# Retention attention feeding a Swish feed-forward block: regrouping a chunk's products and writing two heads into the halves of one bank

## The chip, the cores and the metric

The kernel runs on one core of a Trainium2 chip. The metric is device time in microseconds (us). The profiler records one execution; its instructions are named by engine: PE (TensorE, matrix products), PEld (its weight loads), DVE (VectorE), ACT (ScalarE), POOL (GpSimd) and SP (the queue that issues most DMAs).

## The reference

```python
# q, k, v: [8 batches, 8 heads, 576 positions, 64]
scale = 1.0 / np.sqrt(D_)
scores = scale * np.matmul(q, k.transpose(0, 1, 3, 2))
gamma = 1.0 - 2.0 ** (-5.0 - np.arange(H, dtype=np.float32))
rel = pos[:, None] - pos[None, :]
Dmat = np.where(rel >= 0, gamma[:, None, None] ** rel[None, :, :], 0.0)
attn = np.matmul(scores * Dmat, v)
x = attn.transpose(0, 2, 1, 3).reshape(B * S, H * D)   # [4608, 512]
h = x @ w_in                                           # [4608, 2048]
out = (h * (1.0 / (1.0 + np.exp(-beta * h)))) @ w_out  # [4608, 512]
```

There is no softmax: the decay splits into a factor of the query's position and one of the key's, so a running state per head carries all earlier positions.

## The kernel before

**The two halves.** The feed-forward half works on 9 blocks of 512 tokens. `up` (L277) multiplies one 128-wide slice of the hidden layer: four products of 512 columns into a bank of tag `mm` (three banks), then a Silu on ACT. `down` (L290) adds four of the 16 products of one 128-token output tile in a bank of the same tag; after the last, DVE copies it out (L302) and SP stores it. A block is 16 steps of `up` and 16 of `down`, each of four products. The attention half works on 40 chunks (8 batches of four chunks of 128 positions and one of 64); all 8 heads of a chunk are done together, in four pairs of 64+64 rows.

**A chunk's steps.** `pre` (L169) scales q and v by the decay and casts k to bf16, on POOL from chunk 4 on (L182, L186, L187). v goes into one of three padded tiles `vpads`: each head has 128 columns there, its 64 own ones at the side that belongs to it in the pair and zeros at the other. `load_next` (L191) asks SP for the three loads of the chunk seven further on. q and k are then transposed, up to chunk 13 by `a_T` (L205: eight PE transposes and an ACT copy, L216), from chunk 14 on by `a_X` (L195), a DMA transpose issued from ACT's queue that goes through the crossbar. `a_sc` (L219) makes the scores: eight products of 64 rows, the two heads of a pair in the upper and the lower half of the PE array (L228); DVE masks them into `R` (L232). `a_st` (L256) adds four products to the state (L266), which ACT copies to `sbd`, two heads on a block diagonal (L272). `a_O` (L235) makes the output in one bank: four products of the state before with q (L244), then eight of `vpads` with `R`, each 128 wide with one half zeros (L249); DVE copies the sum to `xT` (L253), which `up` reads.

**The order.** It is written by hand. [...] A list `fill` of `up` and `down` steps is merged with timed steps of the chunks: `merged` (L307) puts a step with time t ahead of fill step number t, rounded up. `attn_steps` (L320) gives the times of a chunk whose time is `at`, with `gap` = 2:

```python
if i < XB:      # XB = 14
    return [(at - 4, F(pre, i)), (at - 3.9, F(load_next, i)), (at, F(a_T, i)), (at + gap, F(a_sc, i)),
            (at + 2 * gap, F(a_st, i)), (at + 2 * gap, F(a_O, i))]
return [(at - 10, F(pre, i)), (at - 9.9, F(load_next, i)), (at - 5, F(a_X, i)), (at + gap, F(a_sc, i)),
        (at + 2 * gap, F(a_st, i)), (at + 2 * gap, F(a_O, i))]
```

So scores come two steps after `at`, state and output two steps after the scores. Chunks 0 to 6 have places written out one by one (L328 to L368), 7 and 8 stand at 23 and 27 of the second list. From chunk 9 on the chunks that block m+1 needs are spread over the 32 steps of block m, four or five to a block; the first such stretch begins at `n1`, where the second part of block 1's `up` begins, with products of 320 columns.

Buffers: `qk` and `qkT` rotate over four, `R` and `sbd` over two, `vpads` over three, the loaded tiles over seven; scores have two banks, output, state and PE transposes one each.

Of the kernel before, what the change touches and what calls it, by code (L numbers as in the profile page):

```python
# [12 lines left out]
BF16 = mybir.dt.bfloat16  # L13
ACT = mybir.ActivationFunctionType
ALU = mybir.AluOpType
# [4 lines left out]
def kernel(  # L20
# [10 lines left out]
    nc = tc.nc  # L31
    B, H, S, D = q.shape
# [3 lines left out]
    P = 128  # L36
    HP = H // 2
    KO = d_model // P
    FO = d_ff // P
    MB = 512  # L40
    NMB = N // MB
# [4 lines left out]
    consts = ctx.enter_context(tc.tile_pool(name="consts", bufs=1))  # L46
# [3 lines left out]
    sb = ctx.enter_context(tc.tile_pool(name="sb", bufs=2))  # L50
# [13 lines left out]
        qkv_tiles[(b, c)] = t  # L64

    NQ = 7
    XB = 14
    order = [(b, c) for b in range(B) for c in range(NC)]
    for b, c in order[:4]:
        load_chunk(b, c)  # L70
# [13 lines left out]
    for h in range(H):  # L84
# [11 lines left out]
    nc.gpsimd.affine_select(out=causal[:], in_=causal[:], pattern=[[1, P]], compare_op=ALU.is_ge,  # L96
                            fill=0.0, base=0, channel_multiplier=-1)

    NV = 3
    vpads = [consts.tile([P, H, P], BF16, name=f"vpad{i}") for i in range(NV)]  # L100

    NS = 2
    sbds = [consts.tile([P, HP, P], BF16, name=f"sbd{i}") for i in range(NS)]
    nc.gpsimd.memset(vpads[0][:], 0.0)
    nc.vector.memset(sbds[0][:], 0.0)
    nc.gpsimd.memset(vpads[1][:], 0.0)
    nc.vector.memset(sbds[1][:], 0.0)


# [57 lines left out]
    live = {}  # L167

    def pre(i):  # L169

        b, c = order[i]
        c0, cL = chunks[c]
        t = qkv_tiles.pop((b, c))
        first = i < 4
        qk = sb.tile([P, 2, H, D], BF16, name="qk", tag="qk", bufs=4)
        qn, kn = qk[:, 0], qk[:, 1]
        vp = vpads[i % NV]

        vp4 = vp.rearrange("p (pr two) (x d) -> p pr (two x) d", two=2, x=2)[:, :, 0::3, :]
        gq_b = gq[:cL, c, :].unsqueeze(2).to_broadcast([cL, H, D])  # L180
        gv_b = gv[:cL, c, :].unsqueeze(2).to_broadcast([cL, H, D])
        (nc.vector if first else nc.gpsimd).tensor_tensor(qn[:cL], t[:cL, 0], gq_b, ALU.mult)  # L182
        if first:
            nc.scalar.copy(kn[:cL], t[:cL, 1])
        else:
            nc.gpsimd.tensor_copy(kn[:cL], t[:cL, 1])  # L186
        nc.gpsimd.tensor_tensor(vp4[:cL], t[:cL, 2].rearrange("p (pr two) d -> p pr two d", two=2),  # L187
                                gv_b.rearrange("p (pr two) d -> p pr two d", two=2), ALU.mult)
        live[i] = dict(qk=qk, qn=qn, kn=kn, vp=vp, vp4=vp4)

    def load_next(i):  # L191
        if i + NQ < len(order):
# [12 lines left out]
    def a_T(i):  # L205
        b, c = order[i]
        c0, cL = chunks[c]
        L = live[i]
        T = psum.tile([P, 2, HP, P], BF16, name="T", tag="T", bufs=1)
        for j, src in enumerate((L["qn"], L["kn"])):  # L210
            for p in range(HP):
                nc.tensor.transpose(T[:, j, p, :cL],  # L212
                                    src[:cL, 2 * p:2 * p + 2, :].rearrange("p h d -> p (h d)"),
                                    ident[:cL, :cL])
        qkT = sb.tile([P, 2, HP, P], BF16, name="qkT", tag="qkT", bufs=4)
        nc.scalar.copy(qkT[:, :, :, :cL], T[:, :, :, :cL])  # L216
        L["qT"], L["kT"] = qkT[:, 0], qkT[:, 1]
# [17 lines left out]
    def a_O(i):  # L235
        b, c = order[i]
        c0, cL = chunks[c]
        L = live[i]
        R, vp = L["R"], L["vp"]
        O = psum.tile([P, HP, P], F32, name="O", tag="O", bufs=1)  # L240
        n = 0
        if c > 0:
            for p in range(HP):
                nc.tensor.matmul(O[:, p, :cL], sbds[(i - 1) % NS][:, p, :], L["qT"][:, p, :cL],  # L244
                                 start=(n == 0), stop=False, skip_group_check=True)
                n += 1
        for j in range(2):
            for p in range(HP):
                nc.tensor.matmul(O[:, p, :cL], vp[:cL, 2 * p + j, :], R[:cL, j, p, :cL],  # L249
                                 start=(n == 0), stop=(j == 1), skip_group_check=True)  # L250
                n += 1
        n0 = b * S + c0
        nc.vector.tensor_copy(xT[:, :, n0:n0 + cL], O[:, :, :cL])  # L253
        del live[i]

    def a_st(i):  # L256
        b, c = order[i]
        c0, cL = chunks[c]
        L = live[i]
        if c == NC - 1:  # L260
            return
        if c == 0:
            state_ps[b] = psum.tile([P, HP, P], F32, name="st", tag="st", bufs=1)
        st = state_ps[b]
        for p in range(HP):
            nc.tensor.matmul(st[:, p, :], L["kn"][:cL, 2 * p:2 * p + 2, :].rearrange("p h d -> p (h d)"),  # L266
                             L["vp4"][:cL, p], start=(c == 0 and p == 0), stop=True,
                             skip_group_check=True)
        sbd = sbds[i % NS]
        for j in range(2):  # L270
            r = slice(j * D, (j + 1) * D)
            nc.scalar.copy(sbd[r, :, j * D:(j + 1) * D], st[r, :, j * D:(j + 1) * D])  # L272
# [34 lines left out]
    def merged(fill, *streams):  # L307

        todo = sorted((x for st in streams for x in st), key=lambda x: x[0])
        for n, f in enumerate(fill):  # L310
            while todo and todo[0][0] <= n:
                todo.pop(0)[1]()
            f()
        for _, step in todo:
            step()

    def F(f, *a):
        return lambda: f(*a)

    def attn_steps(i, at, gap=2.0):  # L320

        if i < XB:
            return [(at - 4, F(pre, i)), (at - 3.9, F(load_next, i)), (at, F(a_T, i)), (at + gap, F(a_sc, i)),
                    (at + 2 * gap, F(a_st, i)), (at + 2 * gap, F(a_O, i))]
        return [(at - 10, F(pre, i)), (at - 9.9, F(load_next, i)), (at - 5, F(a_X, i)), (at + gap, F(a_sc, i)),
                (at + 2 * gap, F(a_st, i)), (at + 2 * gap, F(a_O, i))]

    warm_up(12)  # L328
    betas()
    pre(0)  # L330
    a_T(0)
    nc.gpsimd.memset(vpads[2][:], 0.0)
    pre(1)
    for i in range(4):
        warm_up(2)
        a_sc(i)
        a_st(i)
        if i < 3:
            a_T(i + 1)
            if i < 2:  # L340
                pre(i + 2)
        else:
            cast_w_in(0)
            warm_up(2)
        a_O(i)

    fill = [F(up, 0, fo) for fo in range(FO)]
# [5 lines left out]
    for i in range(5):  # L353
# [7 lines left out]
    fill = [F(up, 1, fo, 0, q1) for fo in range(FO)]  # L361
    fill += [F(down, 0, ms, f0) for f0 in range(0, FO, 4) for ms in range(3)]
    fill += [F(down, 0, 3, f0) for f0 in range(0, FO, 4)]
    n1 = len(fill)
    fill += [F(up, 1, fo, q1, MB - q1) for fo in range(FO)]
    fill += [F(down, 1, ms, f0) for ms in range(MB // P) for f0 in range(0, FO, 4)]
    streams = [[(4, F(cast_w_out, 0)), (10, F(cast_w_out, 1)), (18, F(cast_w_out, 2)), (21, F(cast_w_out, 3))],
               [(0, F(a_T, 6)), (4, F(a_sc, 6)), (8, F(a_st, 6)), (8, F(a_O, 6))],  # L368
               attn_steps(7, 23), attn_steps(8, 27)]
    done = 9  # L370
    need = lambda m: min(len(order), next((i + 1 for i, (b, c) in enumerate(order)
                                          if b * S + chunks[c][0] + chunks[c][1] >= (m + 1) * MB), len(order)))
    todo = list(range(done, need(2)))
    streams += [attn_steps(i, n1 + n * 30 / len(todo)) for n, i in enumerate(todo)]
    done = need(2)
    for m in range(2, NMB):
        base = len(fill)
        fill += [F(up, m, fo) for fo in range(FO)]
        fill += [F(down, m, ms, f0) for ms in range(MB // P) for f0 in range(0, FO, 4)]
        if m + 1 < NMB:  # L380
            todo = list(range(done, need(m + 1)))
            streams += [attn_steps(i, base + n * 31 / len(todo)) for n, i in enumerate(todo)]
            done = need(m + 1)
    merged(fill, *streams)


# [28 lines left out]
```

## Time and profile before

| What | us |
|---|---|
| median of the runs (3 runs: 326.5 to 329.17) | 327.55 |
| the profiled execution, its own time | 327.24 |
| its span, first to last instruction | 325.5 |
| PE busy | 311.7 (96%) |
| ACT busy | 141.6 (44%) |
| DVE busy | 114.4 (35%) |
| POOL busy | 113.3 (35%) |

A line of a timeline has the start, the time from first start to last end, engine, line, operation and count; consecutive equal instructions are merged. Products on PE are pipelined, so the end of a group overlaps the start of the next: what a group costs is the distance from its start to the next group's start. "PEld" rows are the weight loads. "ACTq" and "SPq" rows are DMA issues, and "to landing" is the time from such an issue until the data are there.

### The profile page before, as it was taken

What the parts mean: (1) busy time and instruction counts of PE and PEld (TensorE: products, weight loads), DVE (VectorE), ACT (ScalarE), POOL (GpSimd) and SP (SyncE); (2) the same over time, 40 slices, a digit from 0 to 9 for tenths busy, and PEclk for the clock granted to TensorE, in tenths of its full rate; (3) what the DMA queues carried; (4) which work ended last, traced back from release to release, by engine and by line L of the source; (5) the groups of instructions that cost most, each with busy time, mean ns of one, the idle gap of its engine ahead of it and who ended that gap; (6) DMA issues with size and microseconds to landing.
All of it is one profiled execution on the core that took longest, in us unless ns stands there. A gap on an engine that the chain in (4) does not pass through costs nothing.

```text
span 325.5 us, 5518 instructions
## 1 busy us (share of the span) xinstructions
PE 311.7 (96%) x2208; PEld 163.8 (50%) x2247; DVE 114.4 (35%) x202; ACT 141.6 (44%) x246; POOL 113.3 (35%) x132
## 2 busy tenths in 40 slices
PE   6779999999999999999999999999999999999995
PEld 2544584566555555544555555544545555544442
DVE  3685273634423244214423343224324432330011
ACT  2567881276237610760076106710662057305700
POOL 5323847974333354333333353333333430000000
PEclk9799999999999999999999999999999999999998
DMA  9999999999974999999999869656315121110011
GB/s 171 218 378 244 256 373 220 206 213 213 266 127 126 166 216 220 163 225 184 254 194 191 174 152 226 117 129 156 89 34 113 67 64 34 49 65 34 0 64 64
DMA packets 146362, 52.54 MB, mean 161 GB/s; under 512 B 137616, under 2 KB 137632, under 8 KB 146336
## 3 DMA queue, kind: packets, MB, share of 16 engines
q1 hardware_dynamic: 121920, 46.15, 63.8%
q10 hardware_dynamic: 24416, 6.04, 11.3%
q8 instruction: 17, 0.28, 0.4%
q14 instruction: 9, 0.07, 0.1%
HBM read 36.71 MB, written 9.44 MB: 142 GB/s over the span
## 4 chain that ended last, share of the span: by engine, by line
PE 91%; DVE 3%; DMA 2%; ACT 1%; issue 1%; ACTq 0%
PE po L296 38%; PE ph L284 37%; PE O L249 5%; PE sc L228 4%; PE st L266 2%; DMA qkT<-qk 2%; PE ph L152 2%; PE O L244 2%; PE T L212 2%; DVE R L232 1%; ACT qkT L216 1%; ACT sbd L272 0%; DVE xT L253 0%; DVE w_in_sb L130 0%; DVE tiny L160 0%
## 5 line engine op out<-in xcount | busy, mean ns | idle before, releaser
L284 PE MATMUL ph<-xT,w_in_sb 128*128 128x512 bf16 (+2 forms) x623 | 131.4, 357 | 2.5 <-DVE xT L253 1.6
L296 PE MATMUL po<-w_out_sb,gT 128*128 128x512 bf16 x556 | 130.2, 379 | 1.1 <-issue 0.2
L286 ACT ACTIVATE gT<-ph,beta_sb 128x512 bf16<-128x512 f32 (+2 forms) x160 | 101.9, 645 | 64.6 <-PE ph L284 48.2
L187 POOL TENSOR_TENSOR vpad<-qkvn,gv 128x512 bf16<-128x512 f32 (+1 forms) x40 | 42.0, 1051 | 135.9 <-issue 93.2
L284 PEld LDWEIGHTS <-w_in_sb 128*128 128x128 bf16 x640 | 59.1, 98 | 58.5 <-issue 1.6
L296 PEld LDWEIGHTS <-gT 128*128 128x128 bf16 x576 | 54.0, 98 | 60.6
L232 DVE TENSOR_TENSOR R<-sc,causal 128x512 bf16<-128x512 f32 (+1 forms) x80 | 47.2, 631 | 92.4 <-PE sc L228 92.2
L272 ACT CAST sbd<-st 64x256 bf16<-64x256 f32 x64 | 23.3, 364 | 77.2 <-PE st L266 76.4
L302 DVE COPY ot<-po 128x512 f32<-128x512 f32 x36 | 24.8, 691 | 66.1 <-PE po L296 63.9
L253 DVE CAST xT<-O 128x512 bf16<-128x512 f32 (+1 forms) x40 | 25.5, 637 | 38.2 <-PE O L249 38.2
L182 POOL TENSOR_TENSOR qk<-qkvn,gq 128x512 bf16<-128x512 f32 (+1 forms) x36 | 37.8, 1051 | 2.1 <-DMA qkvn<-in_q_dram 1.6
L249 PE MATMUL O<-R,vpad 128*128 128x128 bf16 (+1 forms) x320 | 23.5, 213 | 1.2 <-DVE R L232 1.2
L216 ACT COPY qkT<-T 128x1024 bf16<-128x1024 bf16 (+1 forms) x14 | 13.3, 950 | 21.8 <-PE T L212 21.7
L186 POOL CAST qk<-qkvn 128x512 bf16<-128x512 f32 (+1 forms) x36 | 21.9, 608 | 1.1 <-DMA qkvn<-in_k_dram 1.1
L249 PEld LDWEIGHTS <-vpad 128*128 128x128 bf16 (+1 forms) x320 | 18.2, 97 | 2.3 <-issue 1.8
L228 PEld LDWEIGHTS <-qkT 64*128 64x128 bf16 (+1 forms) x320 | 8.9, 98 | 17.7 <-issue 11.4
L228 PE MATMUL sc<-qkT 64*128 64x128 bf16 (+1 forms) x320 | 15.4, 217 | 0.9 <-ACT qkT L216 0.4
L266 PEld LDWEIGHTS <-qk 128*128 128x128 bf16 x128 | 9.5, 99 | 6.6 <-issue 0.2
L266 PE MATMUL st<-vpad,qk 128*128 128x128 bf16 x128 | 12.6, 222 | 0.1
L212 PE MATMUL T<-ident,qk 128*128 128x128 bf16 (+1 forms) x112 | 8.7, 224 | 3.1 <-DVE qk L182 3.0
L244 PE MATMUL O<-qkT,sbd 128*128 128x128 bf16 (+1 forms) x128 | 11.5, 212 | 0.0
L212 PEld LDWEIGHTS <-qk 128*128 128x128 bf16 (+1 forms) x112 | 7.2, 103 | 5.1 <-DVE qk L182 3.1
(38 smaller groups left out, 59.1 us busy)
## 6 DMA issues: line engine op xcount, KB each, us to landing
out_dram<-ot SPq DMA_DIRECT2D x36, 256.0 KB, 2.4
qkvn<-in_q_dram SPq DMA_DIRECT2D x32, 256.0 KB, 4.7
qkvn<-in_k_dram SPq DMA_DIRECT2D x32, 256.0 KB, 5.0
qkvn<-in_v_dram SPq DMA_DIRECT2D x32, 256.0 KB, 5.3
wt<-in_moe_w_in_dram SPq DMA_DIRECT2D x4, 1024.0 KB, 10.4
wt<-in_moe_w_out_dram SPq DMA_DIRECT2D x4, 1024.0 KB, 10.6
qkvn<-in_q_dram SPq DMA_DIRECT2D x8, 128.0 KB, 4.7
qkvn<-in_k_dram SPq DMA_DIRECT2D x8, 128.0 KB, 4.3
```

The lines of the kernel that those rows point to most:

```text
L182: (nc.vector if first else nc.gpsimd).tensor_tensor(qn[:cL], t[:cL, 0], gq_b, ALU.mult)
L187: nc.gpsimd.tensor_tensor(vp4[:cL], t[:cL, 2].rearrange("p (pr two) d -> p pr two d", two=2), gv_b.rearrange("p (pr two) d -> p pr two d", ...
L228: nc.tensor.matmul(sc[j][:cL, p, :cL], L["kT"][r, p, :cL], L["qT"][r, p, :cL], start=True, stop=True, skip_group_check=True)
L232: nc.vector.tensor_tensor(R[:cL, j, :, :cL], sc[j][:cL, :, :cL], m_b, ALU.mult)
L249: nc.tensor.matmul(O[:, p, :cL], vp[:cL, 2 * p + j, :], R[:cL, j, p, :cL], start=(n == 0), stop=(j == 1), skip_group_check=True)
L253: nc.vector.tensor_copy(xT[:, :, n0:n0 + cL], O[:, :, :cL])
L266: nc.tensor.matmul(st[:, p, :], L["kn"][:cL, 2 * p:2 * p + 2, :].rearrange("p h d -> p (h d)"), L["vp4"][:cL, p], start=(c == 0 and p == 0 ...
L272: nc.scalar.copy(sbd[r, :, j * D:(j + 1) * D], st[r, :, j * D:(j + 1) * D])
L284: nc.tensor.matmul(ph[:, :tn], w_in_sb[:, ko, fo * P:(fo + 1) * P], xT[:, ko, x0:x0 + tn], start=(ko == 0), stop=(ko == KO - 1))
L286: nc.scalar.activation(gT[:, fo, t0:t0 + tn], ph[:, :tn], ACT.Silu, scale=beta_sb[:, fo:fo + 1])
L296: nc.tensor.matmul(po[:], gT[:, fo, ms * P:(ms + 1) * P], w_out_sb[:, fo, :], start=(fo == 0), stop=(fo == FO - 1))
L302: nc.vector.tensor_copy(ot, po[:])
```

## The change

1. **Padded v is gone.** `vpads`, its three memsets and the strided write are removed. `pre` writes v into `vn`, [128, 8 heads, 64], from a pool of four. `a_st` reads pairs of heads from `vn`.
2. **Output products are 64 wide.** Head j of a pair writes PSUM partitions j·64 to j·64+63, so the product uses 64 columns of the array instead of 128. From chunk 9 on the two heads of a pair follow each other (j = 0, 1, 0, 1, ...); up to chunk 8 all of j = 0 come first. The products with the state now come after them, still 128 wide.
3. **New grouping from chunk 9 on.** One group holds the scores of chunk i, then the output and the state of chunk i-1. A chunk that needs PE transposes has `pre` seven steps and `a_T` three steps ahead of its group; the others keep `pre` at ten and `a_X` at five steps ahead.
4. **Crossbar transposes from chunk 11 on** instead of 14.
5. **One chunk more ahead:** the groups in block m run up to chunk `need(m+1)`, so that the last output needed is in the block before; they are spread over 31 steps (30 before in the first stretch).

```diff
-    vpads = [consts.tile([P, H, P], BF16, name=f"vpad{i}") for i in range(NV)]
...
+        vn = sb.tile([P, H, D], BF16, name="vn", tag="vn", bufs=4)
...
-        nc.gpsimd.tensor_tensor(vp4[:cL], t[:cL, 2].rearrange("p (pr two) d -> p pr two d", two=2),
-                                gv_b.rearrange("p (pr two) d -> p pr two d", two=2), ALU.mult)
+        nc.gpsimd.tensor_tensor(vn[:cL], t[:cL, 2], gv_b, ALU.mult)
...
+        for j, p in [(n // HP, n % HP) if i < 9 else (n % 2, n // 2) for n in range(H)]:
+            nc.tensor.matmul(O[j * D:(j + 1) * D, p, :cL], vn[:cL, 2 * p + j, :], R[:cL, j, p, :cL],
+                             start=(p == 0), stop=(c == 0), skip_group_check=True)
         if c > 0:
             for p in range(HP):
                 nc.tensor.matmul(O[:, p, :cL], sbds[(i - 1) % NS][:, p, :], L["qT"][:, p, :cL],
-                                 start=(n == 0), stop=False, skip_group_check=True)
-        for j in range(2):
-            for p in range(HP):
-                nc.tensor.matmul(O[:, p, :cL], vp[:cL, 2 * p + j, :], R[:cL, j, p, :cL],
+                                 start=False, stop=True, skip_group_check=True)
...
+    C0 = done
+    XB = 11
+    def cluster(i, at):
+        last = len(order) - 1
+        st = []
+        if i <= last:
+            if i < XB:
+                st += [(at - 7, F(pre, i)), (at - 6.9, F(load_next, i)), (at - 3, F(a_T, i))]
+            else:
+                st += [(at - 10, F(pre, i)), (at - 9.9, F(load_next, i)), (at - 5, F(a_X, i))]
+            st += [(at, F(a_sc, i))]
+        if C0 <= i - 1 <= last:
+            st += [(at, F(a_O, i - 1)), (at, F(a_st, i - 1))]
+        return st
+    for m in range(1, NMB - 1):
+        base = n1 if m == 1 else len(fill)
...
+        todo = list(range(done, need(m + 1) + 1))
+        streams += [cluster(i, base + n * 31 / len(todo)) for n, i in enumerate(todo)]
+        done = need(m + 1) + 1
```

More of the change, by code (lines that the diff above doesn't have):

```diff
@@ L66 @@
     NQ = 7
-    XB = 14
     order = [(b, c) for b in range(B) for c in range(NC)]
@@ L97 @@
                             fill=0.0, base=0, channel_multiplier=-1)
-    NV = 3
-    vpads = [consts.tile([P, H, P], BF16, name=f"vpad{i}") for i in range(NV)]
     NS = 2
     sbds = [consts.tile([P, HP, P], BF16, name=f"sbd{i}") for i in range(NS)]
-    nc.gpsimd.memset(vpads[0][:], 0.0)
     nc.vector.memset(sbds[0][:], 0.0)
-    nc.gpsimd.memset(vpads[1][:], 0.0)
     nc.vector.memset(sbds[1][:], 0.0)
@@ L176, in pre @@
         qn, kn = qk[:, 0], qk[:, 1]
-        vp = vpads[i % NV]
-        vp4 = vp.rearrange("p (pr two) (x d) -> p pr (two x) d", two=2, x=2)[:, :, 0::3, :]
+        vn = sb.tile([P, H, D], BF16, name="vn", tag="vn", bufs=4)
         gq_b = gq[:cL, c, :].unsqueeze(2).to_broadcast([cL, H, D])
@@ L186, in pre @@
             nc.gpsimd.tensor_copy(kn[:cL], t[:cL, 1])
-        nc.gpsimd.tensor_tensor(vp4[:cL], t[:cL, 2].rearrange("p (pr two) d -> p pr two d", two=2),
-                                gv_b.rearrange("p (pr two) d -> p pr two d", two=2), ALU.mult)
-        live[i] = dict(qk=qk, qn=qn, kn=kn, vp=vp, vp4=vp4)
+        nc.gpsimd.tensor_tensor(vn[:cL], t[:cL, 2], gv_b, ALU.mult)
+        live[i] = dict(qk=qk, qn=qn, kn=kn, vn=vn)
     def load_next(i):
@@ L238, in a_O @@
         L = live[i]
-        R, vp = L["R"], L["vp"]
+        R, vn = L["R"], L["vn"]
         O = psum.tile([P, HP, P], F32, name="O", tag="O", bufs=1)
-        n = 0
+        for j, p in [(n // HP, n % HP) if i < 9 else (n % 2, n // 2) for n in range(H)]:
+            nc.tensor.matmul(O[j * D:(j + 1) * D, p, :cL], vn[:cL, 2 * p + j, :], R[:cL, j, p, :cL],
+                             start=(p == 0), stop=(c == 0), skip_group_check=True)
         if c > 0:
@@ L244, in a_O @@
                 nc.tensor.matmul(O[:, p, :cL], sbds[(i - 1) % NS][:, p, :], L["qT"][:, p, :cL],
-                                 start=(n == 0), stop=False, skip_group_check=True)
-                n += 1
-        for j in range(2):
-            for p in range(HP):
-                nc.tensor.matmul(O[:, p, :cL], vp[:cL, 2 * p + j, :], R[:cL, j, p, :cL],
-                                 start=(n == 0), stop=(j == 1), skip_group_check=True)
-                n += 1
+                                 start=False, stop=True, skip_group_check=True)
         n0 = b * S + c0
         nc.vector.tensor_copy(xT[:, :, n0:n0 + cL], O[:, :, :cL])
-        del live[i]
     def a_st(i):
@@ L266, in a_st @@
             nc.tensor.matmul(st[:, p, :], L["kn"][:cL, 2 * p:2 * p + 2, :].rearrange("p h d -> p (h d)"),
-                             L["vp4"][:cL, p], start=(c == 0 and p == 0), stop=True,
+                             L["vn"][:cL, 2 * p:2 * p + 2, :].rearrange("p h d -> p (h d)"), start=(c == 0 and p == 0), stop=True,
                              skip_group_check=True)
@@ L320, in attn_steps @@
     def attn_steps(i, at, gap=2.0):
[L322 to L325, printed above, removed]
+        return [(at - 4, F(pre, i)), (at - 3.9, F(load_next, i)), (at, F(a_T, i)), (at + gap, F(a_sc, i)),
                 (at + 2 * gap, F(a_st, i)), (at + 2 * gap, F(a_O, i))]
@@ L331 @@
     a_T(0)
-    nc.gpsimd.memset(vpads[2][:], 0.0)
     pre(1)
@@ L372 @@
                                           if b * S + chunks[c][0] + chunks[c][1] >= (m + 1) * MB), len(order)))
[L373 to L377, printed above, removed]
+    C0 = done
[14 more added lines that the diff above has]
+        base = n1 if m == 1 else len(fill)
+        if m > 1:
+            fill += [F(up, m, fo) for fo in range(FO)]
+            fill += [F(down, m, ms, f0) for ms in range(MB // P) for f0 in range(0, FO, 4)]
+        todo = list(range(done, need(m + 1) + 1))
+        streams += [cluster(i, base + n * 31 / len(todo)) for n, i in enumerate(todo)]
+        done = need(m + 1) + 1
+    for m in range(NMB - 1, NMB):
         fill += [F(up, m, fo) for fo in range(FO)]
         fill += [F(down, m, ms, f0) for ms in range(MB // P) for f0 in range(0, FO, 4)]
[L380 to L383, printed above, removed]
     merged(fill, *streams)
```

## The prediction

> **What bounds the kernel now.** I read the busy totals first, then the chain of work that ended last, then PE's timeline in one stretch of the middle.
>
> ```profile
> span 325.5 us, 5518 instructions
> ...
> PE 311.7 (96%) x2208; PEld 163.8 (50%) x2247; DVE 114.4 (35%) x202; ACT 141.6 (44%) x246; POOL 113.3 (35%) x132
> ...
> PE 91%; DVE 3%; DMA 2%; ACT 1%; issue 1%; ACTq 0%
> ```
>
> PE is 96% busy and 91% of the chain; from 24 us on hardly anything else appears in it. So an edit is worth what it takes from PE's own sequence, unless PE begins to wait. The timeline of PE around chunk 29's scores and chunk 28's output gives the prices:
>
> ```profile
> 205.13 0.59 PE L284 MATMUL ph<-xT,w_in_sb 128*128 128x512 bf16 x2
> 205.66 0.40 PE L228 MATMUL sc<-qkT 64*128 64x128 bf16 x8
> 205.99 1.90 PE L284 MATMUL ph<-xT,w_in_sb 128*128 128x512 bf16 x8
> 207.73 0.39 PE L266 MATMUL st<-vpad,qk 128*128 128x128 bf16 x4
> 207.95 0.39 PE L244 MATMUL O<-qkT,sbd 128*128 128x128 bf16 x4
> 208.18 0.61 PE L249 MATMUL O<-R,vpad 128*128 128x128 bf16 x8
> 208.62 0.38 PE L284 MATMUL ph<-xT,w_in_sb 128*128 128x512 bf16 x1
> ```
>
> Distances between starts: a 512-column product (205.99 to 207.73 over 8) costs 0.216, so a fill step of four 0.865. Four 128-column products (207.73 to 207.95) cost 0.22, eight outputs (208.18 to 208.62) 0.45: 0.056 each. The scores are eight products of 64 rows, two at a time. Four pairs should take 0.22, but from the end of the `up` product before (205.13 + 2 x 0.216 = 205.56) to the next one (205.99) 0.43 pass. The other 0.2 is the way into and out of the halved array, 0.095 each.
>
> The 64-position chunk has the price of 64-wide weight loads, two tiles at a time (weight loads, then PE):
>
> ```profile
> 213.89 0.20 PEld L228 LDWEIGHTS <-qkT 64*64 64x64 bf16 x8 [0.42 <-issue]
> ...
> 213.90 0.31 PE L228 MATMUL sc<-qkT 64*64 64x64 bf16 x8
> ```
>
> Eight loads in 0.20, one of which takes 0.1: about 0.03 per pair of loads, less than the 0.056 of a 128-column product.
>
> Then the crossbar transposes, by stretch (70 to 200 us, then 200 to 290):
>
> ```profile
> L201 ACTq DMA_TRANSPOSE qkT<-qk x15: 1210/1249/1561, 97.6 to 198.9; - x15
> ...
> DMA to landing us min/median/max: 2.7/4.6/7.1
> ...
> L201 ACTq DMA_TRANSPOSE qkT<-qk x12: 1211/1248/1303, 198.9 to 278.3; - x12
> ...
> DMA to landing us min/median/max: 2.6/3.1/5.5
> ```
>
> Alone it lands in about 3; beside loads in 4.6 and up to 7.1. PE waited for one, chunk 20's: issued at 140.67, right behind a chunk's loads, scores at 147.54.
>
> ```profile
> 139.58 1.24 SPq L63 DMA_DIRECT2D qkvn<-in_v_dram  x1
> ...
> 140.67 1.27 ACTq L201 DMA_TRANSPOSE qkT<-qk  x1
> ...
> 147.54 0.40 PE L228 MATMUL sc<-qkT 64*128 64x128 bf16 x8 [0.39 <-DMA qkT<-qk]
> ```
>
> **What the Trainium skill says.** "TensorEngine Tiling (Array Packing)", Key Properties: changing the tiling mode drains TensorE, and different tiles work in parallel. The trace agrees, at 0.095 a change, for row halves. The same page, Restrictions: column tiling rules out fast weight load. "TensorE: Matmul & The Clock Gate", section LDWEIGHTS, prices an ordinary load at columns/1.2 ns; my estimate from it is 0.053 for 64 columns. The loads above beat that. "Trainium Kernel Development and Optimization", Key Constraints: DMAs of all issuing queues share the same 16 engines and interleave; the landing times above fit.
>
> **The change, part by part.**
>
> *Groups from chunk 9 on.* Before, a batch of five chunks costs PE: first chunk 0.42 + 0.22 + 0.45 = 1.09; three chunks 0.42 + 0.22 + 0.22 + 0.45 = 1.31 each; the 64-position chunk 0.34 for scores and 0.54 for its output (which also changes the mode twice), 0.88. Sum 5.90. After: five groups with three mode changes each (in, row halves to column halves, out) 15 x 0.095 = 1.43; scores in pairs 4 x 0.22 + 0.14 = 1.02; outputs in pairs the same, 1.02; products with the state 3 x 0.22 + 0.12 = 0.78; state 4 x 0.22 = 0.88. Sum 5.13. The gain is 0.77 a batch and 4.8 for 31 chunks. Column halves side by side are not in this trace. The bounds are 0.22 for eight (taken, since the row halves do it and the loads fit) and 0.45 (no overlap; see the rivals). The inner change of mode lies between 0 and 0.2; I take 0.095, which leaves 3 us either way for 32 groups.
>
> *Transposes of chunks 11 to 13.* PE loses three groups of eight at 0.45: -1.35. ACT exchanges three copies of 1.01 for three issues of 1.25; it is 44% busy. The DMA engines get three more transfers.
>
> *Chunks up to 8.* Here the outputs stay one after the other, and the group has two changes of mode more: 0.19 each for chunks 6, 7, 8 = 0.57. Where PE waits for the mask, the products with the state used to run inside that wait and now follow it. Chunk 5: 0.095 + 0.22 = 0.32. Chunk 4: its old output already changed mode; +0.1. Chunks 1 and 2: 0.32 each, less 0.1 in which PE waits for the ACT copy anyway, so 0.46 for both; chunk 0 has slack, chunk 3 hides behind DVE's weight casts. Together +1.45.
>
> *At nothing:* the three memsets (0.95 each; POOL waits for v's landing there), POOL's write of v (same 512 elements a row, 1.04), its wait for the padded tile (now for a buffer of four; POOL 35% busy), DVE's mask and copy back to back (2.0; one `down` tile takes 3.5 and there are three `mm` banks), ACT's state copies (0.74 at the group's end; Silu takes 0.69 of each 0.865). The loads, asked for some steps earlier, sit on SP, which runs in order with the output stores; they come seven chunks ahead (chunk 24's were issued at 125.7, its scores at 177.7), so this is hidden too. If that cover went, POOL's scaling would be late, then the transpose.
>
> *The wait that gets shorter cover.* `a_X` stood seven fill steps and one chunk's output group ahead of the scores: 6.8 to 7.2 in the trace where `up` runs beside it. Now it stands five steps ahead with no group between: 5 x 0.865, less 0.2 for ACT's lag, plus 0.1 = 4.2. For chunk 11 those five are `up` steps of 320 columns, 0.55 each: 2.6; for chunk 12 some 3.5. Where `down` runs, ACT is idle and issues earlier; I estimate 4.7 to 6. Behind a late transpose stand the scores and, PE being in order, everything else. The cost is at least 0. At most, the eight transposes issued beside `up` before 200 us landed after 3.1, 5.2, 4.9, 6.8, 7.1, 4.3, 4.8 and 5.5; above 4.2 that is 9.2, or 1.15 each. Ten come with the short lead in the loaded stretch (chunks 11, 12, 15, 16, 17, 20, 21, 24, 25, 26): 11.5, and 1.5 more for chunk 11.
>
> I take 1.0. A wait on PE also gives the loads time, so the next transpose meets fewer of them. Loads that are on time are asked for five steps ahead of the transpose, so most have landed; in the trace SP was late (chunk 21's load issued at 115.5). This is the weakest step. Chunk 20's wait of 0.4 I count as gone in the same breath.
>
> *Sum* against the profiled execution's 327.24 (span and 1.7 around it): -4.8 - 1.35 + 1.45 - 0.4 + 1.0 = 323.1. The median stands 0.3 above that execution: **323.4**.
>
> **The rivals.**
>
> *Slower: the crossbar becomes the wait.* The place is the scores of chunks 11 to 26; the price is the upper bound above, 13 instead of 1.0, giving 335. For it: five of those eight landings are 4.8 or more. Against: in the second stretch the median is 3.1. It decides from about 0.8 per short-lead transpose (330.8).
>
> *In between:* waits of 4 to 5 eat the gain: 327.
>
> *Columns do not overlap*, because the ordinary loads follow one another or the halves share a path: eight outputs keep 0.45, which returns 6.2 x (4 x 0.22 + 0.12) = 6.2: 329.6. Against it speaks the pair price of 64-wide loads; for it, only that no column half is in the trace.
>
> **How the numbers follow.** Forecast 0.52 (own range 321.5 to 325.5), crossbar wait 0.25 (330 to 337), in between 0.16, columns 0.07. A measurement of this kernel tells about 1% from no change: 3.3, so the borders are 324.3 and 330.8. Faster: most of the forecast, 0.45. Slower: the crossbar case and a little of the columns, 0.27. Same: 0.28. Cases of both signs count, so the range goes from 321.5 up to 332, which leaves out most of the crossbar case's upper part and a little below.
>
> **What would show it.** Right: groups of scores, output and state with output products starting in pairs every 0.056; about 0.095 at each change; PE's waits for `qkT` below 2 in all; none of the transposes of chunks 11 to 13 left on PE; landings still 3 to 5. Wrong: `sc` waiting for the DMA of `qkT` in many groups with landings of 5 and more; output products 0.056 apart one by one; Silu late behind a transpose issue that itself waits on ACT's queue.

## The result, and the profile after

| | before | after |
|---|---|---|
| median of the runs, us | 327.08 | 343.94 |
| runs, us | 326.5 to 329.17 | 340.62, 343.01, 344.88 |
| profiled execution: its time, its span, us | 327.24, 325.5 | 343.01, 341.3 |
| mean clock granted to PE in it | 0.992 | 0.970 |

The changed kernel is slower, by a ratio of 1.047 (95% interval 1.0369 to 1.0571). One more run, of 799.69 us at a full clock, counts in the median shown but is left out of the ratio. A fourth run of the kernel before, 326.61, has moved its median from 327.55.

The head of the changed kernel's page: span, busy time with its share and number of instructions, the clock in forty slices, and the chain of work that ended last.

```profile
span 341.3 us, 5525 instructions
...
PE 316.5 (93%) x2223; PEld 158.8 (47%) x2223; DVE 110.5 (32%) x202; ACT 137.7 (40%) x243; POOL 110.0 (32%) x129
...
PEclk9599999995999989899999999999999999999999
...
PE 37%; DMA 5%; issue 1%; POOL 1%; DVE 0%; SPq 0%
```

PE's share falls from 96% to 93%, so it now stands still for more of the span. Its busy time still rises by 4.8 us, although it has less to do: the digits 5 and 8 in the clock row say that part of it ran slowly. In the chain DMA has 5% where it had 2%. (The chain was followed back only to 187 us, so its shares don't add up to the span.)

What PE waited for (us in total, times, the longest), in the changed kernel:

```profile
PE sc L219 <- DMA qkT<-qk: 14.0, 9, 3.7
```

The scores waited 14.0 us for crossbar transposes; before it was 0.4, at chunk 20 only. Chunk by chunk, taking the gap between the end of the product before, at its even pace (0.216 for 512 columns), and the scores, less 0.1 for the change of mode, it is chunk 11 3.8, 15 1.9, 16 2.0, 18 3.4, 25 1.3, 26 1.2, and 1.1 for four more; 14.7 in all.

The transposes of the changed kernel from 70 to 200 us and from 200 to 320 us (name, count, duration of the issue in ns, first and last start; then the time to landing):

```profile
L192 ACTq DMA_TRANSPOSE qkT<-qk x16: 1210/1249/1395, 73.1 to 194.2; - x16
...
DMA to landing us min/median/max: 3.1/5.3/8.4
...
L192 ACTq DMA_TRANSPOSE qkT<-qk x13: 1211/1248/1313, 200.8 to 290.2; - x13
...
DMA to landing us min/median/max: 2.7/3.1/4.7
```

In the loaded stretch half of them take over 5.3 to land. The lead they were given beside `up` was the one that the prediction worked out: where nothing waits, 4.1 to 4.2 us lie between issue and scores (chunk 21: 157.2 to 161.3). Chunk 11 had 3.2, chunk 12 4.7, and where `down` runs it is mostly 5 to 6.7. Chunk 18, which had 5.1, shows what stands beside a late one (timeline of all engines, changed kernel):

```profile
126.56 0.37 SPq L63 DMA_DIRECT2D qkvn<-in_v_dram  x1
...
127.02 1.00 SPq L291 DMA_DIRECT2D out_dram<-ot  x2
...
127.98 1.30 ACTq L192 DMA_TRANSPOSE qkT<-qk  x1
128.11 0.42 SPq L63 DMA_DIRECT2D qkvn<-in_q_dram  x1
...
128.59 1.11 SPq L63 DMA_DIRECT2D qkvn<-in_k_dram  x1
...
136.44 0.61 PE L219 MATMUL sc<-qkT 64*128 64x128 bf16 x8 [3.38 <-DMA qkT<-qk]
```

Three loads of 256 KB and two stores of 256 KB are issued within about 2 us around the transpose, which lands 8.4 after its issue.

The clock. PE's timeline around chunk 11's wait, then the windows of PE in the changed kernel (length, busy time and count, granted clock, DMA share, GB/s):

```profile
75.07 1.25 PE L271 MATMUL ph<-xT,w_in_sb 128*128 128x320 bf16 x8 [0.44 <-ACT gT L273]
80.03 0.61 PE L219 MATMUL sc<-qkT 64*128 64x128 bf16 x8 [3.71 <-DMA qkT<-qk]
80.56 0.64 PE L234 MATMUL O<-R,vn 128*64 128x128 bf16 x8
```

```profile
80.00:84.00 4.00, 3.97 (x30) 0.50 0.02 6
...
134.00:142.00 8.00, 5.56 (x38) 0.79 0.97 192
142.00:200.00 58.00, 55.34 (x390) 1.00 1.10 199
200.00:341.30 141.30, 137.21 (x884) 1.00 0.38 85
```

After eight `up` products nothing is left to do ahead of the scores, and PE stands for 3.7 us. Behind the wait the scores cost 0.53 (80.03 to 80.56) where they cost 0.33 before: PE runs at half speed, 0.50 in the window from 80 us. The window with chunk 18 has 0.79. From 142 us on the clock is full. The clock's record has half speed for 6.8 us from 78.4, for 3.4 from about 119.3 (behind chunk 16's wait of 2.0) and for 3.4 from 136.4, and for 6.8 at the start, where before had 3.4. The Trainium skill, "TensorE: Matmul & The Clock Gate", Part 1, says that an idle window of about 3.4 us halves PE's clock and that the windows run freely. The trace agrees on the size and the windows: 0.50, in pieces of 3.41 whose starts lie 12 and 5 whole pieces apart (78.36, 119.32, 136.39). It doesn't agree that the whole window must be idle, and the measurement decides: in the piece ahead of 119.32 PE stood for chunk 16's 2.0 only.

The sum for the span, +15.8: waits 14.7 - 0.5 = +14.2; the clock, 0.030 x 341.3 - 0.008 x 325.5 = 7.6, of which 0.8 lies in a wait, leaves +6.8; the rest is -5.2. Of the 6.8, 6.0 lies behind the waits (half of 6.8 + 3.4 + 3.4, less the 0.8); the start has 1.7 more than before and the end 0.8 less. The start's longer piece isn't behind a late transpose (e5 below has it too, in an execution of 322.54). The prediction's terms for the products, -4.8 - 1.35 + 1.45 - 0.4, make -5.1; that this comes so close is partly luck, as two of the terms were off in opposite directions (see below).

A group of the changed kernel, on PE's timeline:

```profile
204.30 1.46 PE L283 MATMUL po<-w_out_sb,gT 128*128 128x512 bf16 x6
205.69 0.40 PE L219 MATMUL sc<-qkT 64*128 64x128 bf16 x8
206.01 0.41 PE L234 MATMUL O<-R,vn 128*64 128x128 bf16 x8
206.36 0.40 PE L238 MATMUL O<-qkT,sbd 128*128 128x128 bf16 x4
206.59 0.39 PE L253 MATMUL st<-vn,qk 128*128 128x128 bf16 x4
206.82 6.21 PE L283 MATMUL po<-w_out_sb,gT 128*128 128x512 bf16 x28
```

From 204.30 + 6 x 0.216 = 205.60 to 206.82 it costs 1.22. The prediction's terms give 3 x 0.095 + 4 x 0.22 = 1.17, and the same work cost 1.31 before. The eight outputs take 0.35 with their change of mode.

### The profile page after: what moved, and what is told of

Read it like the earlier page. It is cut to its first block, busy times and chain, and to the rows that moved or that the text cites. A ratio compares the mean times of both kernels' runs of the same rounds, so it can differ in the third digit from the quotient of the medians.

```text
span 341.3 us, 5525 instructions
## 1 busy us (share of the span) xinstructions
PE 316.5 (93%) x2223; PEld 158.8 (47%) x2223; DVE 110.5 (32%) x202; ACT 137.7 (40%) x243; POOL 110.0 (32%) x129
## 5 line engine op out<-in xcount | busy, mean ns | idle before, releaser
L273 ACT ACTIVATE gT<-ph,beta_sb 128x512 bf16<-128x512 f32 (+2 forms) x160 | 99.5, 645 | 52.0 <-PE ph L271 47.0
L271 PEld LDWEIGHTS <-w_in_sb 128*128 128x128 bf16 x640 | 61.5, 99 | 62.6 <-issue 4.4
L283 PEld LDWEIGHTS <-gT 128*128 128x128 bf16 x576 | 55.8, 99 | 64.0 <-issue 1.1
L179 POOL TENSOR_TENSOR vn<-qkvn,gv 128x512 bf16<-128x512 f32 (+1 forms) x40 | 41.7, 1041 | 37.1 <-DMA qkvn<-in_v_dram 16.9
L234 PE MATMUL O<-R,vn 128*64 128x128 bf16 (+1 forms) x320 | 17.8, 227 | 1.1 <-DVE R L223 1.1
L207 ACT COPY qkT<-T 128x1024 bf16<-128x1024 bf16 (+1 forms) x11 | 10.3, 933 | 12.8 <-PE T L203 12.6
L234 PEld LDWEIGHTS <-vn 128*64 128x64 bf16 (+1 forms) x320 | 11.2, 113 | 6.7 <-issue 3.6
L253 PE MATMUL st<-vn,qk 128*128 128x128 bf16 x128 | 13.4, 231 | 0.0
L146 PE MATMUL ph<-warm 128*128 128x512 bf16 x22 | 8.7, 537 | 1.2 <-DVE warm L75 1.2
L203 PE MATMUL T<-ident,qk 128*128 128x128 bf16 (+1 forms) x88 | 7.2, 231 | 2.3 <-DVE qk L174 2.3
## 6 DMA issues: line engine op xcount, KB each, us to landing
wt<-in_moe_w_out_dram SPq DMA_DIRECT2D x4, 1024.0 KB, 10.2
```

What stands on the lines that cost most here:

```text
L179: nc.gpsimd.tensor_tensor(vn[:cL], t[:cL, 2], gv_b, ALU.mult)
L234: nc.tensor.matmul(O[j * D:(j + 1) * D, p, :cL], vn[:cL, 2 * p + j, :], R[:cL, j, p, :cL], start=(p == 0), stop=(c == 0), skip_group_check ...
L271: nc.tensor.matmul(ph[:, :tn], w_in_sb[:, ko, fo * P:(fo + 1) * P], xT[:, ko, x0:x0 + tn], start=(ko == 0), stop=(ko == KO - 1))
L273: nc.scalar.activation(gT[:, fo, t0:t0 + tn], ph[:, :tn], ACT.Silu, scale=beta_sb[:, fo:fo + 1])
L283: nc.tensor.matmul(po[:], gT[:, fo, ms * P:(ms + 1) * P], w_out_sb[:, fo, :], start=(fo == 0), stop=(fo == FO - 1))
```

## The experiments

Three theories stood at the start. A: the gain on PE is there, and the short lead of the transposes eats it, as in the slower rival. B: the added transposes of chunks 11 to 13 delay the DMA queue. C: the new groups cost PE more than the old ones. Each ratio is to runs of the kernel before that were made beside that experiment.

| kernel | lead, steps | median, us | ratio to before (95%) | scores' wait for `qkT` | landing 70 to 200 us, min/median/max |
|---|---|---|---|---|---|
| e4_before_short | 4 | 344.59 | 1.0532 (1.0494 to 1.057) | 11.7 | 2.7/4.0/7.9 |
| e2_xb14 | 5 | 334.36 | 1.0222 (1.0205 to 1.0239) | 12.2 | 3.1/5.0/7.5 |
| e8_lead7 | 7 | 325.50 | 0.9945 (0.9922 to 0.9968) | 4.9 | 2.6/5.9/7.5 |
| e1_lead9 | 9 | 322.51 | 0.986 (0.984 to 0.9881) | 1.1 | 4.0/5.6/8.7 |
| e3_lead9_xb14 | 9 | 323.30 | 0.9888 (0.9874 to 0.9903) | 0 | 2.7/5.4/7.8 |
| e9_fewloads | 5 | 325.20 | 0.9929 (0.9903 to 0.9956) | 0.5 | 2.6/3.1/4.4 |
| e5_oneafterother | 9 | 322.67 | 0.9854 (0.9822 to 0.9886) | 0.2 | 3.8/6.3/9.4 |
| e6_oldplaces | as before | 326.52 | 0.9973 (0.9945 to 1.0001) | 0 | 2.8/4.8/6.3 |
| e7_best | 9 | 323.49 | 0.988 (0.9847 to 0.9913) | 1.9 | |

Steps are fill steps from the transpose's place to the scores' place. The kernel before has 7, with an output group in between, as in e4.

**e1_lead9**: the changed kernel with the transposes four steps earlier. Scaling and loads, which must come before them, go three steps earlier too; e4 below moves the transposes alone.

```diff
-                st += [(at - 10, F(pre, i)), (at - 9.9, F(load_next, i)), (at - 5, F(a_X, i))]
+                st += [(at - 13, F(pre, i)), (at - 12.9, F(load_next, i)), (at - 9, F(a_X, i))]
```

> The changed kernel with the crossbar transposes nine fill steps ahead of their scores instead of five, and scaling and loads three steps earlier, all else as changed. Theory A (the shorter lead is the whole loss): the lead goes from 4.2 us to about 7.7, longer than nearly every landing, so PE's waits for the transposed q and k fall from 14.7 us to under 2, the clock drops that follow long waits go too, and the time is 322 to 325 us. Theory B (the three added transposes in the loaded stretch delay the DMA queue): waits stay at 8 us or more and the time above 334. Theory C (the new groups themselves cost PE more than the old ones): time about 330 with few waits.

It is 1.4% faster than before, where theory C had about 330. PE's waits, and its windows in the loaded stretch:

```profile
PE sc L219 <- DMA qkT<-qk: 1.1, 1, 1.1
```

```profile
100.00:130.00 30.00, 30.00 (x228) 1.00 1.30 230
130.00:160.00 30.00, 30.00 (x191) 1.00 1.16 212
160.00:200.00 40.00, 40.00 (x293) 1.00 1.18 217
```

PE is busy for all of 100 to 200 us at a full clock, although the transposes land no sooner:

```profile
L192 ACTq DMA_TRANSPOSE qkT<-qk x19: 1210/1248/2547, 70.1 to 187.6; - x19
...
DMA to landing us min/median/max: 4.0/5.6/8.7
```

So it isn't the landing that changed but the lead over it, now 8.4 us or more from chunk 15 on. Chunk 11 alone, with 5.6, still waits, for a landing of 6.6. That speaks for A and against C.

**e2_xb14**: the changed kernel with PE transposes for chunks 11 to 13 again, as before the change.

```diff
-    XB = 11
+    XB = 14
```

> The changed kernel with crossbar transposes from chunk 14 on, as before, and the lead of five steps kept. Theory A: chunks 11 to 13 go back to PE (+1.3 us) and chunk 11's wait of 3.9 us goes, but the waits of chunks 15 to 29 (about 10.8 us) stay; 336 to 341 us. Theory B: waits go almost wholly, about 324 us. Theory C: about 331.

```profile
PE sc L219 <- DMA qkT<-qk: 12.2, 9, 2.4
```

The waits go down by 1.8 only: without chunk 11's, other chunks wait more. The longest is now 2.4 and the clock loses 0.012 x 336.1 = 4.0 instead of 10.2. Together that is 8.0, less 1.35 for PE's own transposes; the profiled executions differ by 5.2 (337.81), the medians by 9.6. Theory B had about 324 and hardly any waits, so it is out as the main cause. But the median also lies under theory A's 336 to 341: with the short lead, the added transposes carry up to 9.6 of the 21.4 us between the changed kernel and e1, through the first long wait and part of the clock's loss.

**e3_lead9_xb14**: both edits together.

> Both: nine steps of lead and crossbar transposes from chunk 14 on. Theory A: like nine steps alone, 1.3 us more for the three transposes on PE, 323 to 326 us. Theory B: like chunk 14 alone. If this one is clearly faster than nine steps alone, the three added transposes cost more than they save even with a long lead.

There is no wait at all, and it stands 0.8 above e1. Three groups of transposes more on PE, priced at 1.35, less e1's wait of 1.1 would give 0.25; the difference is inside the spread of e1's runs (321.43 to 323.13). So the crossbar for chunks 11 to 13 is worth about its wait.

**e4_before_short**: the kernel before, none of whose products is changed, with the short lead alone.

```diff
-        return [(at - 10, F(pre, i)), (at - 9.9, F(load_next, i)), (at - 5, F(a_X, i)), (at + gap, F(a_sc, i)),
+        return [(at - 10, F(pre, i)), (at - 9.9, F(load_next, i)), (at - 2, F(a_X, i)), (at + gap, F(a_sc, i)),
```

> The kernel before with the one edit that its crossbar transposes are issued two steps ahead of at instead of five, so four fill steps and one output group ahead of the scores: a lead of about 4.2 us, as in the changed kernel, with the old groups. Theory A: PE waits 8 to 14 us for the transposes and the time is 336 to 345 us. Theory C: the lead alone costs little, at most 3 us, 327 to 330.

```profile
PE sc L228 <- DMA qkT<-qk: 11.7, 7, 3.2
```

A loss of this size, 17.6, appears without the change's products. The lead is mostly 3.3 to 4.1 here, a little shorter than in the changed kernel. The lead is shown to be enough to cause the loss.

**e8_lead7**: the changed kernel with the transposes at seven steps.

```diff
-                st += [(at - 10, F(pre, i)), (at - 9.9, F(load_next, i)), (at - 5, F(a_X, i))]
+                st += [(at - 11, F(pre, i)), (at - 10.9, F(load_next, i)), (at - 7, F(a_X, i))]
```

> The changed kernel with seven steps of lead, about 5.9 us. Landings in the loaded stretch run from 3 to 8, so a part of the waits should stay: 2 to 5 us, 324 to 328. If the loss only needs the landing's median of about 4.6 covered, 322.5 as with nine steps.

Not quite half of e1's gain over before is there. Chunk 11 still waits 2.9 of the 5.4 (gaps less 0.1). (The profiled execution took 326.91, 1.4 above the median.) Five, seven and nine steps give 14.0, 4.9 and 1.1 of waiting.

**e9_fewloads**: the changed kernel, with its short lead, without the loads of chunks 14 to 39. From chunk 14 on it works on the tiles of chunks 10 to 13 again, so it doesn't compute the reference; it is there for its times alone.

```diff
-        t = qkv_tiles.pop((b, c))
+        t = qkv_tiles[order[i if i < 14 else 10 + i % 4]]
...
-        if i + NQ < len(order):
+        if i + NQ < 14:
```

> The changed kernel with its short lead of 4.2 us, but chunks from 14 on use the q, k and v of chunks 10 to 13 again, and the loads of chunks 14 to 39 are left out. If the transposes land late because loads and stores share the DMA engines with them, they land in about 3 us, PE waits for them under 1.5 us from chunk 14 on, and the time is 321 to 327. If the lateness lies in the transposes or their issue alone, the waits stay and the time is above 334.

```profile
L192 ACTq DMA_TRANSPOSE qkT<-qk x19: 1210/1249/2235, 74.6 to 199.1; - x19
...
DMA to landing us min/median/max: 2.6/3.1/4.4
```

The landings come down to those of the second half of the kernel, and the waits go. So it is the loads that make a transpose late; whether by their bytes alone or by when they are issued isn't told apart. It doesn't reach e1's time; the view of waits has 2.7 us for `xT` where e1 has 1.1, which is part of that.

**e5_oneafterother**: e1, with all products of the lower half of the array ahead of those of the upper half in every chunk, to see what alternating them is worth.

```diff
-        for j, p in [(n // HP, n % HP) if i < 9 else (n % 2, n // 2) for n in range(H)]:
+        for j, p in [(n // HP, n % HP) for n in range(H)]:
```

> Nine steps of lead (322.5 us), but the 64-wide output products of all chunks in the order that chunks up to 8 have: the four of the lower half first, then the four of the upper. If the halves work side by side only when their products alternate, each full chunk loses 0.22 us: 31 chunks, 6.2 us, 328 to 329. If they did not work side by side anyway, no change, 322.5.

The time is e1's, but not for the reason that was expected with it: the halves do work side by side, whichever order the program has. PE's timeline in it:

```profile
201.08 0.42 PE L234 MATMUL O<-R,vn 128*64 128x128 bf16 x8
201.44 0.40 PE L238 MATMUL O<-qkT,sbd 128*128 128x128 bf16 x4
201.67 0.39 PE L253 MATMUL st<-vn,qk 128*128 128x128 bf16 x4
```

The eight outputs take 0.36 again, with the change of mode. Their recorded starts lie in pairs 0.013 apart (201.083 and 201.096, 201.163 and 201.176, and so on). Four products of one half alone do not pair. In chunk 2 of the changed kernel the upper half waits for its mask, and each half's four take 0.38, where four full-width products take 0.39:

```profile
18.80 0.38 PE L234 MATMUL O<-R,vn 128*64 128x128 bf16 x4
19.40 0.38 PE L234 MATMUL O<-R,vn 128*64 128x128 bf16 x4 [0.21 <-DVE R L223]
```

Their starts are 0.055 apart. So a pair is one product of each half.

**e6_oldplaces**: the kernel before with the unpadded 64-wide outputs alone, scores, state and output at their old places.

```diff
-        for j in range(2):
-            for p in range(HP):
-                nc.tensor.matmul(O[:, p, :cL], vp[:cL, 2 * p + j, :], R[:cL, j, p, :cL],
-                                 start=(n == 0), stop=(j == 1), skip_group_check=True)
-                n += 1
+        for j, p in [(n // HP, n % HP) if i < 9 else (n % 2, n // 2) for n in range(H)]:
+            nc.tensor.matmul(O[j * D:(j + 1) * D, p, :cL], vn[:cL, 2 * p + j, :], R[:cL, j, p, :cL],
+                             start=(p == 0), stop=(c == 0), skip_group_check=True)
```

> The kernel before with only the 64-wide output products from the unpadded v, paired from chunk 9 on; old places, old lead, crossbar transposes from chunk 14. Summing as in the prediction, a full chunk saves 0.22 in the products and pays two changes of mode, 0.19; the early chunks lose about 1 us. So 326 to 327.5, no gain: the gain needs scores and output side by side, which saves one change a chunk and both extra ones of the 64-position chunk. Against this, if the pairs alone carry the gain: 322 to 324.

Alone it gives nothing that can be measured. That fits the sum expected: two more changes of mode take back what the halves side by side save.

**e7_best**: e1, with the old order of products in chunks up to 5, alternating halves from chunk 6 on, and the crossbar from chunk 12 on.

```diff
-        for j, p in [(n // HP, n % HP) if i < 9 else (n % 2, n // 2) for n in range(H)]:
+        early = i < 6
+        if early:
+            with_state(True)
+        for j, p in [(n // HP, n % HP) if early else (n % 2, n // 2) for n in range(H)]:
...
-    XB = 11
+    XB = 12
```

> Nine steps of lead, crossbar transposes from chunk 12 on (chunk 11's wait of 1.15 us goes, one transpose of 0.45 comes back to PE), products with the state first again for chunks up to 5, so that they run inside the wait for the mask (0.7 us), and pairs already from chunk 6 on (0.22 each for three chunks). Together about 2 us under nine steps alone: 320 to 321.5 us, ratio to the kernel before 0.980 to 0.984. If the early chunks hide these edits, 322.

It is no faster than e1, against what was expected. By chunk 9's scores it is 0.6 ahead (66.3 against 66.9), but e1's profiled execution had 3.4 us at half speed at its start and this one none, so the 0.6 can't be put down to the edits. Then its first transpose, chunk 12's, waits 1.9 where e1's waits 1.1, and PE has a group of transposes more. e1_lead9 has the lowest median, 322.51 (e5's 322.67 is level with it), and beats both kernels.

## Why the prediction was wrong

**The step that failed** is "I take 1.0" for the wait that gets shorter cover. The runs show 14.7 in its place, and 6.0 of lost clock behind it, which no case had a price for. The slower rival had the mechanism, nearly the place (scores of chunks 11 to 26) and 335; what it lacked to 343 is mostly the clock. Its point of decision, 0.8 for each of ten short-lead transposes, was passed: at the ten chunks that it counted the waits are 10.9 in all, or 1.1 each, inside its bound of 13. What lifts the sum above the bound is chunk 18's 3.4, which it did not count: `down` runs there, the lead was 5.1, within the 4.7 to 6 that it estimated, and the landing took 8.4. (Its 1.15 for each left out one transpose issued beside `up` before 200 us, chunk 14's with 2.7; with it, 9.2 over nine would be 1.0.)

The readings behind the 1.0 were mostly right. The lead was: 4.2 worked out, 4.1 to 4.2 measured (for chunks 11 and 12, 2.6 and 3.5 worked out, 3.2 and 4.7 measured). The landings beside `up` were on the page, 4.6 in the middle and up to 7.1. What set the number aside were two arguments. The first was that a wait on PE gives the loads time, so that the next transpose meets fewer. In the result the landings are 5.3 in the middle, no shorter than before, and with the waits gone (e1) 5.6: they follow the loads in flight, as e9 shows with 3.1, and not what PE does. The second was that loads are asked for early and so have landed. The waits of SP in the changed kernel, 70 to 200 us, speak against it:

```profile
SPq L63 <- DMA qkT<-qk: 58.1, 12, 11.0
```

SP held loads back behind a transpose's landing 12 times, and issued them behind it; that loads and transposes meet so often because of this fits, but no run tests it apart. The wait was in the trace of before too (26.7 us, 5 times, on SP) and wasn't read. Why a load waits for a transpose that it shares no buffer with stays open.

**The groups** were right in direction and too large in size. Five groups in e1 (those from 136.69 to 167.70) cost 0.79 + 1.00 + 1.23 + 1.23 + 1.14 = 5.39, from the end of the `up` or `down` product ahead, at its even pace, to the start of the next one; the prediction had 5.13. A batch before costs 5.94, measured the same way. The gain is 0.55 a batch, about 3.4 for 31 chunks instead of 4.8. The columns do overlap, so that rival falls.

**Chunks up to 8** were priced too high, +1.45. At the end of chunk 8's output the kernels stand at 65.22 (before) and 65.96 (e1), 0.7 apart; 0.3 of it is chunk 9's transposes on PE, which stand ahead of this point in e1 (62.99 to 63.31) and behind it before. That leaves 0.4. The price of 0.45 for outputs one after the other was wrong: they overlap there as well, 65.44 to 65.80 in the changed kernel.

**Transposes off PE** (-1.35): the runs with and without them, e1 and e3, lie too close together to size it. **Chunk 20's wait** (-0.4, counted as gone) is still 0.3 in the changed kernel and gone in e1.

**What was put at nothing** held for the memsets, POOL's write, DVE's back-to-back work and ACT's copies: e1 carries all of them and PE is without a gap from 100 to 200 us. It didn't hold for SP's loads: they were hidden for their own chunks, but not from the transposes beside them.

Taken without the wait, the prediction's median was 322.4; e1, where the wait is nearly gone, has 322.51. That is closer than its terms deserve: the groups brought 1.4 less than predicted and the early chunks cost 1.0 less.

## What to carry to other kernels

When an edit takes cover from a DMA, compare the new lead with the upper part of the landings in the very stretch where it will stand, and assume that the excess is paid for each transfer unless a run shows otherwise. Here moving nothing but the transposes four steps ahead, and their scaling and loads three, turned a loss of 4.7% into a gain of 1.4%. A wait of 2 to 4 us on PE can cost more than itself, because the clock may fall behind it: it did behind 2.0, 3.4 and 3.7 in the changed kernel, and did not behind 3.2 in e4 or 2.8 in e8.

## What the runs showed of the hardware

- Output products of the two column halves run side by side even where the program has all of one half first (e5: 0.36 for eight, change of mode included, starts in pairs 0.013 apart). The Trainium skill, "TensorEngine Tiling (Array Packing)", Key Properties, says that different tiles work in parallel, which agrees; "TensorE: Matmul & The Clock Gate", Part 3, says that products start strictly in program order, which these starts don't fit. Chunk 8 of the changed kernel shows it directly. There too the program has one half first, and of its eight products the first and the second to start (65.440, 65.454) carry a wait for a semaphore; in chunk 2, where the upper half comes late, it is the first and the fifth. So the upper half's first product, the fifth in the program, started second; here the measurement decides against the page. What picks the order isn't shown.
- Three changes of mode in a row cost little more each than one alone: 0.10 into the row halves, 0.10 from row to column halves and 0.13 out of them (the group from 205.60; 0.22 taken off for each set of products).
- One transpose of the same 128-position size lands after 3.0 to 9.4 us over these runs (the 9.4 is chunk 23's in e5). The loads decide: with the short lead and the stretch the same, the middle is 5.3 with them and 3.1 without (e9).
- Whether the clock falls depends on where a wait lies, not only on its length. Chunk 16's 2.0 lay within one piece of 3.41 (115.91 to 119.32), and half speed followed. The longest wait of e4, 3.2, was split by the border of two pieces (134.88, counted back from the pieces at 179.25 and 220.21) into 1.4 and 1.8, and the clock stayed full. A sharp limit doesn't follow: e6 has a piece with 2.0 of standing, from 21.7 (counted back from 325.53), and full clock behind it.
